# Linear attention and a gated long convolution on one core: orbit order split by parity, scoring tiles of 128 columns, last batch stored tile by tile

## The chip, the cores and the metric

The kernel runs on one core of a Trainium2 chip. The metric is device time in microseconds for one launch. The kernel before has a median of 273.19 us over three runs (269.62, 273.19 and 273.72 us). "PE" is TensorE, "PEld" its weight loads, "DVE" VectorE, "ACT" ScalarE, "POOL" GpSimd and "SP" SyncE, whose queue starts DMAs.

## The reference

Eight batches, eight heads, 576 positions, 64 features per head. A linear attention with cosine weighting feeds a gated convolution over the positions:

```python
def phi(x, c, s):
    r = np.maximum(x, 0.0)
    return np.concatenate([r * c, r * s], axis=-1)
q_p, k_p = phi(q, cos_w, sin_w), phi(k, cos_w, sin_w)
kv  = np.einsum('bhsf,bhsd->bhfd', k_p, v)
num = np.einsum('bhsf,bhfd->bhsd', q_p, kv)
den = np.einsum('bhsf,bhf->bhs', q_p, np.sum(k_p, axis=2))[..., None] + 1e-06
x   = (num / den)                       # then [b, 576, 512]
...
x1, x2, x3 = split(x @ w_proj, 3)       # 512 columns each
x2_conv = irfft(rfft(x2, axis=1) * rfft(filter_fft, axis=0), n=576, axis=1)
out = (x1 * x2_conv * x3) @ w_out
```

## The kernel before

**Work of one batch.** POOL's queue loads q, k and v and casts them to fp16 (`load_qk`). DVE makes the rectified, weighted `kp` and `qp` (`emit_phi`), ACT copies v into `va`. `emit_kv` multiplies them per head into `kvs` (128 features by 65 columns, the last for the denominator; 48 matmuls at L519). `emit_qt` transposes `qp` into `qpt`, 128 features by 8 heads by 576 positions: by PE for batches 0 and 1, and from batch 2 on by four DMA transposes on SP's queue (L531).

`emit_num` (L547) is the scoring step. For each pair of heads it writes one PSUM unit. For each head it goes over six tiles of 96 positions; a tile takes every second column of `qpt` from a block of 192 columns as the stationary operand (96 columns) and streams 65 columns of `kvs` (L558). That is 48 matmuls a batch. DVE then adds epsilon, takes the reciprocal and multiplies into `att` (L564, L567, L568).

`emit_fx` (L573) turns the positions into sums over orbits, the first stage of a discrete Fourier transform by hand. The helper `fold` (L581) takes 128 features of one `att` tile as the stationary operand (96 by 128) and streams the table `fm` (96 by 192). Two tiles, e = 0 and 1, share 384 columns of a PSUM bank: the view `(g o e)` has e innermost, so each matmul writes 192 values, two apart. There are 24 such matmuls a batch (16 into `fx`, 8 into `fxc`), and ACT casts the sums into the SBUF tile `fx` (L593, L601).

`emit_x2`, `emit_dft` (L609, L625) project the second third, transform it and multiply it by the filter's spectrum; `emit_gate` (L647) projects the first and last third, and DVE multiplies them into `g` (L671); `emit_inv` (L680) transforms back, ACT casts into `eq` (L693). `emit_y` (L698) combines even and odd halves on DVE: per 128 features four `eo` instructions of 128 by 144 (L705), two of 128 by 288 (L708, L709), and a product with `g` (L710). `emit_out` (L717) multiplies by `w_out` in five tiles of 128 positions (L728), scales into `os` (ACT at L733; in the last batch ACT at L735 and DVE through the helper at L100) and stores rows to DRAM (L748): nine stores a batch of up to 96 rows, on SP's queue, in the last two batches partly on ACT's.

**Order of the work.** The code is written as a pipeline (L841 to L896): iteration b scores and folds batch b+1, transforms and gates batch b, and stores batch b-1. A scheduler orders each engine's list at build time from there. All PSUM results share one pool of four units of two banks (`unit`, L64): a matmul group that starts a new unit waits until ACT or DVE has emptied an earlier one.

**Tables.** `emit_fm`, `emit_fwd_tables` and the index row `sr_i` compute the fold table and the transform tables on the chip at the start; their formulas follow the order in which `fx` holds the positions.

Of the kernel before, what the change touches and what calls it, by code (L numbers as in the profile page):

```python
# [11 lines left out]
FP32 = mybir.dt.float32  # L12
FP16 = mybir.dt.float16
# [4 lines left out]
def kernel(  # L18
# [8 lines left out]
    out: bass.AP,  # L27
):


# [60 lines left out]
    feo = setupp.tile([NP, 2, 3, DM], FP16, tag="feo", name="feo")  # L91
    qpt_buf = [consts.tile([128, NH, S], FP16, tag=f"qpt{i}", name=f"qpt{i}") for i in range(1)]
    va_buf = [consts.tile([NP, NH, NJ, 66], FP16, tag=f"va{i}", name=f"va{i}") for i in range(2)]
# [242 lines left out]
    def emit_fwd_tables():  # L336
# [3 lines left out]
        tsc(half, p, 47.5, AL.is_gt)  # L340
        u = small("u16")
        rnd(u, p, 1.0 / 16.0, -15.0 / 32.0)
        j = small("jr")
        nc.vector.scalar_tensor_tensor(
            out=j, in0=half, scalar=-3.0, in1=u, op0=AL.mult, op1=AL.add
        )
        w = small("w2s")

        tsc(w, p, 12.0, AL.mult, 1.0, AL.add)
        nc.vector.scalar_tensor_tensor(out=w, in0=u, scalar=-192.0, in1=w, op0=AL.mult, op1=AL.add)  # L350
        nc.vector.scalar_tensor_tensor(out=w, in0=j, scalar=2.0, in1=w, op0=AL.mult, op1=AL.add)
        tn = setupp.tile([NP, 3, NP], I32, tag="tn_big", name="tn_fwd")
# [86 lines left out]
    def emit_h(bls):  # L439
# [8 lines left out]
        for bl in bls:  # L448
# [16 lines left out]
            nc.vector.tensor_copy(out=h3[:, bl, 2], in_=h3[:, bl, 1])  # L465
        if 2 not in bls:
            return
        u = unit("h_nyq")
        for j in range(3):
            nc.tensor.matmul(  # L470
                u[0:1, 0], alt[:, j % 2 : j % 2 + 1], feo[:, 0, j], start=(j == 0), stop=(j == 2)
            )
        nc.scalar.activation(out=h3[0:1, 0, 2], in_=u[0:1, 0], func=AF.Copy, scale=1.0 / S)

# [52 lines left out]
    def emit_qt(b, hp):  # L527
        qp, qpt = qp_t[b], qpt_buf[0]
        hsl = slice(2 * hp, 2 * hp + 2)
# [17 lines left out]
    def emit_num(b, hp, wm=0):  # L547
# [6 lines left out]
        for hh in range(2):  # L554
            h = 2 * hp + hh
            for t in range(NT):
                c0 = 2 * NP * (t // 2) + t % 2
                nc.tensor.matmul(  # L558
                    u[0:NP, hh, ds(t * 65, 65)], qpt[:, h, c0 : c0 + 2 * NP - 1 : 2],
                    kvs[:, h // 4, ds((h % 4) * 65, 65)], start=True, stop=True,  # L560
                )
# [13 lines left out]
    def emit_fx(b, cs=range(NC), wm=0):  # L575
# [5 lines left out]
        def fold(dst, j, c):  # L581
            for e in range(2):
                nc.tensor.matmul(  # L583
                    dst[:, 0:384].rearrange("p (g o e) -> p g o e", o=8, e=2)[:, :, :, e],
                    att[:, 2 * j + e, ds(c * 128, 128)], fm[0:NP], start=True, stop=True,
                )
# [60 lines left out]
    def emit_gate(b, c):  # L647
# [22 lines left out]
        for hf in range(2):  # L670
            mark["g", b, c] = nc.vector.tensor_tensor(  # L671
                out=(g[:, c, 0:HS] if hf == 0 else g[:, c, HS:S][:, ::-1]).rearrange(
                    "p (j i o) -> p j i o", j=3, i=6
                ),
                in0=x3s[:, hf, 0:HS].rearrange("p (i j o) -> p j i o", i=6, j=3),
                in1=x1s[:, hf].rearrange("p (i j o) -> p j i o", i=6, j=3),
                op=AL.mult,
            )
# [19 lines left out]
    def emit_y(b, c):  # L698
        eq, y, g = moe[b]["eq", c], moe[b]["y"], moe[b]["g"]
        eo = late["p"].tile([128, 2, HS], FP16, tag="eo", bufs=2, name=f"eo{b}_{c}")  # L700
        eoh = eo.rearrange("p a (j x) -> p a j x", j=3)
        eqj = eq.rearrange("p a b (j x) -> p a b j x", j=3)
        for x, op in ((0, AL.add), (1, AL.subtract)):
            for a in range(2):
                nc.vector.tensor_tensor(  # L705
                    out=eoh[:, a, :, ds(48 * x, 48)], in0=eqj[:, a, 0], in1=eqj[:, a, 1], op=op
                )
        nc.vector.tensor_tensor(out=y[:, c, 0:HS], in0=eo[:, 0], in1=eo[:, 1], op=AL.add)  # L708
# [5 lines left out]
    OG = ((0, 1), (2, 3), (4,))  # L714
    OL = ((4,), (0, 1), (2, 3))

    def emit_out(b, grps=OG):  # L717
        y = moe[b]["y"]
        ov = out[b].rearrange("(p j) n -> j p n", j=6)
        for grp in grps:  # L720
            ng = len(grp)
            os_ = late["p"].tile(
                [128, ng, DM], FP32, tag=f"os{ng}", bufs=2 * ng, name=f"os{b}_{grp[0]}"
            )
            u = unit(f"out{b}_{grp[0]}")
            for x, t in enumerate(grp):
                for c in range(NC):
                    nc.tensor.matmul(  # L728
                        u[:, x], y[:, c, ds(OT[t], 128)], wo16[:, c],
                        start=(c == 0), stop=(c == NC - 1),  # L730
                    )
            if b < B - 1:
                nc.scalar.mul(out=os_[:, 0 : len(grp)], in_=u[:, 0 : len(grp)], mul=OUTSC)  # L733
            else:
                nc.scalar.mul(out=os_[:, 0], in_=u[:, 0], mul=OUTSC)  # L735
                if len(grp) > 1:
                    tsc(os_[:, 1], u[:, 1], OUTSC, AL.mult)
            for t in grp:
                lo, hi_ = (OT[t], OT[t] + 128) if t < 4 else (512, 576)
                x = lo  # L740
                while x < hi_:
                    jb = x // NP
                    e = min(hi_, (jb + 1) * NP)
                    p_a, p_b = x - jb * NP, e - jb * NP
                    src = os_[x - OT[t] : e - OT[t], t - grp[0]]
                    dst = ov[jb, p_a:p_b]
                    q_ = nc.scalar if b >= B - 2 and t % 2 == 1 else nc.sync
                    q_.dma_start(out=dst, in_=src)  # L748
                    x = e

# [90 lines left out]
    for b in range(1, B + 1):  # L841
# [47 lines left out]
        for x in range(4):  # L889
            if b >= 1 and x < 3 and (b != B - 1 or x > 0):  # L890
                emit_out(b - 1, ((OG if b < B else OL)[x],))
        if n + 1 < B:
# [34 lines left out]
```

## Time and profile before

| What | Value |
|---|---|
| median of three runs | 273.19 us (269.62 to 273.72) |
| the profiled execution: its own time, and its span | 272.69 us, 270.9 us |
| PE busy | 248.9 us, 92% of the span, 2265 matmuls |
| PE weight loads busy | 180.0 us, 66% |
| DVE busy | 219.5 us, 81%, 790 instructions |
| ACT busy | 188.0 us, 69%, 268 instructions |
| POOL busy | 35.5 us, 13% |
| chain that ended last | PE 80%, DVE 10%, ACT 4%, DMA 3% |
| granted PE clock, mean over the span | 0.98 |

The profile is one execution. Busy time is an average over stages with different limits, so the stages have to be read one by one: the chain of waits tells which engine's work follows itself without a gap, and the table of windows gives the busy time of each engine in a stretch. Matmuls overlap each other, so the mean duration of one is longer than its share of the time: what a matmul costs on the chain is the length of its stretch divided by the number in it.

### The profile page before, as it was taken

What the parts mean: (1) busy time and instruction counts of PE and PEld (TensorE: products, weight loads), DVE (VectorE), ACT (ScalarE), POOL (GpSimd) and SP (SyncE); (2) the same over time, 40 slices, a digit from 0 to 9 for tenths busy, and PEclk for the clock granted to TensorE, in tenths of its full rate; (3) what the DMA queues carried; (4) which work ended last, traced back from release to release, by engine and by line L of the source; (5) the groups of instructions that cost most, each with busy time, mean ns of one, the idle gap of its engine ahead of it and who ended that gap; (6) DMA issues with size and microseconds to landing.
All of it is one profiled execution on the core that took longest, in us unless ns stands there. A gap on an engine that the chain in (4) does not pass through costs nothing.

```text
span 270.9 us, 6009 instructions
## 1 busy us (share of the span) xinstructions
PE 248.9 (92%) x2265; PEld 180.0 (66%) x2265; DVE 219.5 (81%) x790; ACT 188.0 (69%) x268; POOL 35.5 (13%) x59
## 2 busy tenths in 40 slices
PE   0389898999889999999999999999999999999991
PEld 0267576756767866785778677867786778756830
DVE  7677889899799879988798969896996597546951
ACT  2244599999778859766886778576966466767630
POOL 8516011413110310030012011000000000000000
PEclk9995999999999999999999999999999999999997
DMA  5999996899997489949996999816600600062045
GB/s 73 184 207 203 207 199 92 95 212 189 142 144 121 47 193 132 196 73 167 175 154 101 150 182 159 124 31 178 142 2 1 173 4 2 0 174 70 12 116 155
DMA packets 60205, 33.75 MB, mean 125 GB/s; under 512 B 39504, under 2 KB 55376, under 8 KB 60176
## 3 DMA queue, kind: packets, MB, share of 16 engines
q0 software_dynamic: 26000, 16.85, 46.0%
q1 hardware_dynamic: 33536, 15.47, 27.5%
q10 hardware_dynamic: 640, 1.05, 1.3%
q8 instruction: 17, 0.28, 0.4%
q14 instruction: 12, 0.10, 0.1%
HBM read 33.69 MB, written 9.44 MB: 159 GB/s over the span
## 4 chain that ended last, share of the span: by engine, by line
PE 80%; DVE 10%; ACT 4%; DMA 3%; issue 1%; POOL 0%; POOLq 0%; ACTq 0%
PE x L658 20%; PE x L618 15%; PE out L728 11%; PE fx L583 7%; PE num L558 6%; PE kv L519 4%; PE dft L633 4%; PE fxc L583 3%; PE inv L689 2%; PE inv L690 2%; DMA vraw<-in_v_dram 2%; DVE kp L102 2%; PE h_ps L457 2%; DVE eo L705 2%; ACT fx L593 1%; PE qt L539 1%
## 5 line engine op out<-in xcount | busy, mean ns | idle before, releaser
L658 PE MATMUL x<-fx,wp 128*128 128x288 f16 x512 | 68.3, 287 | 0.6 <-ACT fx L593 0.6
L658 PEld LDWEIGHTS <-wp 128*128 128x128 f16 x512 | 51.6, 101 | 14.0
L618 PE MATMUL x<-wp,fx 128*96 128x512 f16 x192 | 46.2, 381 | 1.0 <-DVE qpt L545 0.9
L593 ACT CAST fx<-fx 128x768 f16<-128x768 f32 x32 | 25.3, 797 | 21.3 <-PE fx L583 21.3
L728 PE MATMUL out<-wo,y 128*128 128x512 f16 x160 | 36.0, 379 | 0.7 <-DVE y L710 0.7
L623 ACT ACTIVATE x2f<-x 96x1024 f16<-96x1024 f32 x24 | 24.6, 1024 | 15.1 <-PE x L618 15.1
L618 PEld LDWEIGHTS <-fx 128*96 128x96 f16 x192 | 22.0, 123 | 15.4 <-issue 1.3
L139 ACT COPY va<-vraw 96x768 f16<-96x768 f16 x32 | 25.2, 832 | 8.7 <-DMA vraw<-in_v_dram 8.7
L568 DVE TENSOR_TENSOR att<-num,rcp 96x768 f16<-96x768 f32 x32 | 30.3, 947 | 0.2
L583 PEld LDWEIGHTS <-att 96*128 96x128 f16 x192 | 24.2, 128 | 9.3 <-DVE att L568 2.5
L583 PE MATMUL fx<-fm,att 96*128 96x192 f16 x128 | 26.6, 364 | 1.5 <-DVE att L568 1.5
L728 PEld LDWEIGHTS <-y 128*128 128x128 f16 x160 | 15.3, 98 | 18.2 <-DVE y L710 1.2
L705 DVE TENSOR_TENSOR eo<-eq 128x144 f16<-128x144 f16 x128 | 22.9, 225 | 5.5 <-ACT eq L693 5.3
L671 DVE TENSOR_TENSOR g<-x,x1s 128x288 f16<-128x288 f32 x48 | 20.4, 448 | 7.9 <-PE x L658 6.9
L558 PEld LDWEIGHTS <-qpt 128*96 128x96 f16 x384 | 21.6, 126 | 6.4 <-issue 2.6
L635 ACT CAST xf<-dft 96x1024 f16<-96x1024 f32 x24 | 24.1, 1006 | 2.1 <-ACT x1s L664 1.9
L519 PE MATMUL kv<-va,kp 96*128 96x65 f16 x384 | 16.6, 199 | 9.6 <-ACT va L139 7.6
L733 ACT ACTIVATE os<-out 128x1024 f32<-128x1024 f32 (+1 forms) x21 | 17.8, 880 | 10.7 <-PE out L728 10.7
L664 ACT CAST x1s<-x 128x576 f16<-128x576 f32 x32 | 20.5, 642 | 4.9 <-PE x L658 2.3
L519 PEld LDWEIGHTS <-kp 96*128 96x128 f16 x384 | 15.3, 102 | 12.7 <-DVE kp L102 10.7
L558 PE MATMUL num<-kvs,qpt 128*96 128x65 f16 x384 | 21.4, 211 | 1.4 <-DVE rcp L567 0.7
L638 DVE TENSOR_TENSOR m<-xf,h 96x1024 f16<-96x1024 f16 x24 | 16.3, 678 | 5.4 <-ACT xf L635 4.7
(191 smaller groups left out, 421.7 us busy)
## 6 DMA issues: line engine op xcount, KB each, us to landing
out_dram<-os SPq DMA_DIRECT2D x22, 192.0 KB, 2.6
kraw<-in_k_dram POOLq DMA_DIRECT2D x7, 576.0 KB, 9.2
vraw<-in_v_dram POOLq DMA_DIRECT2D x7, 576.0 KB, 8.0
out_dram<-os SPq DMA_DIRECT2D x20, 128.0 KB, 2.4
qraw<-in_q_dram POOLq DMA_DIRECT2D x8, 288.0 KB, 5.4
qraw<-in_q_dram POOLq DMA_DIRECT2D x12, 144.0 KB, 5.4
wp<-in_moe_w_proj_dram POOLq DMA_DIRECT2D x3, 512.0 KB, 11.6
out_dram<-os SPq DMA_DIRECT2D x22, 64.0 KB, 2.0
```

The lines of the kernel that those rows point to most:

```text
L139: nc.scalar.copy(out=va_buf[b % 2][:, hs, :, 0:D], in_=raw_t[(b, "v")][:, hs].rearrange("p h (j d) -> p h j d", j=NJ),)
L519: nc.tensor.matmul(u[:, h // 4, ds((h % 4) * 65, 65)], kp[:, j, h].rearrange("p a b -> p (a b)"), va[:, h, j, 0:65], start=(j == 0), stop= ...
L558: nc.tensor.matmul(u[0:NP, hh, ds(t * 65, 65)], qpt[:, h, c0 : c0 + 2 * NP - 1 : 2], kvs[:, h // 4, ds((h % 4) * 65, 65)], start=True, sto ...
L568: mark["att", b, hp] = nc.vector.tensor_tensor(out=att[:, :, ds(hp * 128, 128)].rearrange("p t (h d) -> p h t d", h=2), in0=nv[:, :, :, 0: ...
L583: nc.tensor.matmul(dst[:, 0:384].rearrange("p (g o e) -> p g o e", o=8, e=2)[:, :, :, e], att[:, 2 * j + e, ds(c * 128, 128)], fm[0:NP], s ...
L593: nc.scalar.copy(out=fx[:, c, :, 0:32].rearrange("p g (j o) -> p j g o", j=2), in_=u[:, :, 0:384].rearrange("p j (g o) -> p j g o", o=16),)
L618: nc.tensor.matmul(u[0:NP, comp], fx[:, c, ds(comp * 6 + 2 * bl, 2)].rearrange("p a b -> p (a b)"), wp16[:, c, ds(DM, DM)], start=(c == 0) ...
L623: mark["x2f", b, bl] = nc.scalar.mul(out=x2f[:, bl], in_=u[0:NP], mul=X2SC)
L635: mark["xf", b, bl] = nc.scalar.copy(out=xf, in_=u[0:NP])
L658: nc.tensor.matmul(u[:, hf, 0:HS], wp16[:, i, ds(w * DM + c * 128, 128)], fx[:, i, ds(12 + 6 * hf, 6)].rearrange("p a b -> p (a b)"), star ...
L705: nc.vector.tensor_tensor(out=eoh[:, a, :, ds(48 * x, 48)], in0=eqj[:, a, 0], in1=eqj[:, a, 1], op=op)
L728: nc.tensor.matmul(u[:, x], y[:, c, ds(OT[t], 128)], wo16[:, c], start=(c == 0), stop=(c == NC - 1),)
```

## The change

**Parity.** The orbit order of the positions is split by parity. In `fold` the view becomes `(g e o)`: each matmul writes 24 runs of 8 adjacent values. `fx` keeps its size, but its 48 places per group stand in another order, so the tables' formulas, the views of `g`, `eo` and the rows of the output follow it. With the new order the four `eo` instructions of 128 by 144 become two of 128 by 288, and an output tile's rows go to DRAM in runs of at most 48 rows (stride 12) where they went in runs of at most 96 (stride 6): 15 stores a batch where there were 9.

**Scoring.** `qpt` becomes one flat tile, and `emit_num` takes 128 stationary columns (every second one, so the last 32 belong to the next tile or the next head) in place of 96, except for the last two tiles of a pair's second head: 40 of the 48 matmuls of a batch have 128 columns and 8 keep 96. The 32 further rows of PSUM that they write are not read.

**Last batch.** Each of the five output tiles of batch 7 gets its own PSUM unit, its own scaling on DVE (`osl`, five buffers) and its own stores, on SP's and ACT's queues, in the order 0 to 4 (before: tile 4 first, then pairs, scaled by ACT and DVE in turn). Batch 6's tiles 2 to 4 store partly by POOL's queue in place of ACT's. The `os` tiles of the other batches have half as many buffers.

**Small things.** The matmuls for the Nyquist row `h_nyq` stand behind the first block of `emit_h` in place of the last; `sr_i` is made by three POOL instructions in place of one; `emit_fwd_tables` has two more column instructions on DVE.

```diff
@@ emit_iotas
-        iota("sr_i", [NP, QS], lambda t: [(t, [[2, 3], [12, NP // 2]], 1, 0)])
+        iota("sr_i", [NP, QS], lambda t: [
+            (t[:, ds(j * 48, 48)], [[12, 2], [192, 3], [24, 8]], 2 * j + 1, 0) for j in range(3)
+        ])
...
@@ emit_num
-                c0 = 2 * NP * (t // 2) + t % 2
+                m = NP if hh and t >= 4 else 128
+                c0 = h * S + 2 * NP * (t // 2) + t % 2
                 nc.tensor.matmul(
-                    u[0:NP, hh, ds(t * 65, 65)], qpt[:, h, c0 : c0 + 2 * NP - 1 : 2],
+                    u[0:m, hh, ds(t * 65, 65)], qpt[:, c0 : c0 + 2 * m - 1 : 2],
                     kvs[:, h // 4, ds((h % 4) * 65, 65)], start=True, stop=True,
                 )
...
@@ fold
-                    dst[:, 0:384].rearrange("p (g o e) -> p g o e", o=8, e=2)[:, :, :, e],
+                    dst[:, 0:384].rearrange("p (g e o) -> p g e o", e=2, o=8)[:, :, e],
                     att[:, 2 * j + e, ds(c * 128, 128)], fm[0:NP], start=True, stop=True,
...
@@ emit_gate
-                    "p (j i o) -> p j i o", j=3, i=6
+                    "p (t i o) -> p t i o", t=6, i=6
                 ),
-                in0=x3s[:, hf, 0:HS].rearrange("p (i j o) -> p j i o", i=6, j=3),
-                in1=x1s[:, hf].rearrange("p (i j o) -> p j i o", i=6, j=3),
+                in0=x3s[:, hf, 0:HS].rearrange("p (i t o) -> p t i o", i=6, t=6),
+                in1=x1s[:, hf].rearrange("p (i t o) -> p t i o", i=6, t=6),
...
@@ emit_y
-            for a in range(2):
-                nc.vector.tensor_tensor(
-                    out=eoh[:, a, :, ds(48 * x, 48)], in0=eqj[:, a, 0], in1=eqj[:, a, 1], op=op
-                )
+            nc.vector.tensor_tensor(
+                out=eoh[:, :, :, x], in0=eqt[:, :, 0], in1=eqt[:, :, 1], op=op
+            )
...
@@ emit_out
+                if last and x:
+                    u = unit(f"out{b}_{t}")
...
+                if last:
+                    tsc(os_[t][:, 0], u[:, x], OUTSC, AL.mult)
...
+                while pos < hi_:
+                    m = pos // 48
+                    e = min(hi_, (m + 1) * 48)
+                    k0 = pos - m * 48
+                    r = 6 * (m % 2) + m // 2
+                    q_ = nc.sync
+                    if m % 2 == 1 and (last or (b == B - 2 and t > 1)):
+                        q_ = nc.scalar if last else nc.gpsimd
+                    q_.dma_start(out=ov[r, k0 : k0 + e - pos], in_=sv[pos - OT[t] : e - OT[t]])
+                    pos = e
```

The order of PE's matmuls in the pipeline's middle is the same in both kernels. Two places move. The first is SP's queue in the middle of the pipeline: the DMA transposes of one batch and, behind them, the stores of another (`os_0`, `os_2` and `os_4` are its scaled tiles). Before:

```order
L531 DMA_TRANSPOSE qpt_90<-qp_2458 128x12x96 x4
L748 DMA out_dram<-os_0_2488 96x512
L748 DMA out_dram<-os_0_2488 32x512
L748 DMA out_dram<-os_0_2488 64x512 x2
L748 DMA out_dram<-os_2_2503 32x512
L748 DMA out_dram<-os_2_2503 96x512 x2
L748 DMA out_dram<-os_2_2503 32x512
L748 DMA out_dram<-os_4_2518 64x512
```

Changed:

```order
L538 DMA_TRANSPOSE qpt_90<-qp_2452 128x12x96 x4
L760 DMA out_dram<-os_0_2483 48x512 x2
L760 DMA out_dram<-os_0_2483 32x512
L760 DMA out_dram<-os_0_2483 16x512
L760 DMA out_dram<-os_0_2483 48x512 x2
L760 DMA out_dram<-os_0_2483 16x512
L760 DMA out_dram<-os_2_2501 32x512
L760 DMA out_dram<-os_2_2501 48x512 x4
L760 DMA out_dram<-os_2_2501 32x512
L760 DMA out_dram<-os_4_2518 16x512
L760 DMA out_dram<-os_4_2518 48x512
```

The four transposes of the next batch now stand behind 15 stores where they stood behind 9.

The second place is the end of the program, on ACT and DVE; `os_..._41xx` and `os_..._42xx` are the scaled tiles of batch 7, `os_2_4126`/`os_4_4141` (changed: `os_2_4116`/`os_4_4133`) those of batch 6. ACT before:

```order
L733 ACTIVATE os_4_4141<-out_4_4142 128x512
L748 DMA out_dram<-os_2_4126 96x512
L748 DMA out_dram<-os_2_4126 32x512
L735 ACTIVATE os_4_4181<-out_4_4182 128x512
L735 ACTIVATE os_0_4189<-out_0_4190 128x512
L748 DMA out_dram<-os_0_4189 64x512 x2
L735 ACTIVATE os_2_4205<-out_2_4206 128x512
L748 DMA out_dram<-os_2_4205 96x512
L748 DMA out_dram<-os_2_4205 32x512
```

ACT changed:

```order
L747 ACTIVATE os_4_4133<-out_4_4132 128x512
L760 DMA out_dram<-os_0_4166 48x512
L760 DMA out_dram<-os_1_4173 48x512
L760 DMA out_dram<-os_1_4173 16x512
L760 DMA out_dram<-os_2_4187 32x512
L760 DMA out_dram<-os_2_4187 48x512
L760 DMA out_dram<-os_3_4194 48x512
L760 DMA out_dram<-os_4_4207 48x512
```

ACT only issues stores there now, and the five scalings stand on DVE behind the last `y`:

```order
L716 TENSOR_TENSOR y_4048<-eo_3_4159 128x288
L717 TENSOR_TENSOR y_4048<-eo_3_4159 128x288
L718 TENSOR_TENSOR y_4048<-y_4048,g_3970 128x576
L102 TENSOR_SCALAR os_0_4166<-out_0_4165 128x512
L102 TENSOR_SCALAR os_1_4173<-out_1_4172 128x512
L102 TENSOR_SCALAR os_2_4187<-out_2_4186 128x512
L102 TENSOR_SCALAR os_3_4194<-out_3_4193 128x512
L102 TENSOR_SCALAR os_4_4207<-out_4_4206 128x512
```

Before, DVE had two of them (`os_0` and `os_2`'s second halves), each behind ACT's half of the same tile.

More of the change, by code (lines that the diff above doesn't have):

```diff
@@ L91 @@
     feo = setupp.tile([NP, 2, 3, DM], FP16, tag="feo", name="feo")
-    qpt_buf = [consts.tile([128, NH, S], FP16, tag=f"qpt{i}", name=f"qpt{i}") for i in range(1)]
+    qpt_buf = [consts.tile([128, NH * S], FP16, tag=f"qpt{i}", name=f"qpt{i}") for i in range(1)]
     va_buf = [consts.tile([NP, NH, NJ, 66], FP16, tag=f"va{i}", name=f"va{i}") for i in range(2)]
@@ L465, in emit_h @@
             nc.vector.tensor_copy(out=h3[:, bl, 2], in_=h3[:, bl, 1])
[L466 to L473, printed above, removed]
+            if bl > 0:
+                continue
+            u = unit("h_nyq")
+            for j in range(3):
+                nc.tensor.matmul(
+                    u[0:1, 0], alt[:, j % 2 : j % 2 + 1], feo[:, 0, j], start=(j == 0), stop=(j == 2)
+                )
+            nc.scalar.activation(out=h3[0:1, 0, 2], in_=u[0:1, 0], func=AF.Copy, scale=1.0 / S)
     kp_t, qp_t, kvs_t, att_t, fx_t, xt_t = {}, {}, {}, {}, {}, {}
```

62 lines of the change are left out of this document (28 added, 34 removed).

## The prediction

> **What bounds the kernel now.** I read the table of windows first, to see which engine fills which stretch, with the stretches cut where the chain of waits changes its engine. The columns are the length, then busy time and instructions of PE, PEld, DVE, ACT and POOL, the granted PE clock, the DMA share and GB/s.
>
> ```profile
> 30.70:44.70 14.00, 12.41 (x125) 10.07 (x126) 13.18 (x51) 12.39 (x21) 1.54 (x2) 1.00 1.05 157
> 44.70:62.00 17.30, 17.30 (x160) 11.18 (x160) 15.87 (x48) 16.91 (x27) 4.49 (x5) 1.00 1.10 159
> 71.00:77.27 6.27, 4.86 (x106) 4.33 (x104) 5.73 (x26) 5.71 (x9) 0.00 (x0) 1.00 0.83 145
> 77.27:99.47 22.20, 22.20 (x202) 16.55 (x200) 21.41 (x75) 17.19 (x25) 2.82 (x4) 1.00 0.76 112
> 99.47:239.28 139.81, 139.81 (x1284) 103.16 (x1282) 115.52 (x372) 100.76 (x135) 8.72 (x12) 1.00 0.65 109
> ...
> 127.74:156.00 28.26, 28.26 (x267) 20.92 (x266) 24.76 (x81) 20.84 (x28) 3.60 (x5) 1.00 1.00 148
> ```
>
> From 77 to 239 us PE has no idle time, at full clock. One batch takes 28.26 us there; DVE is busy for 24.76 and ACT for 20.84 of it. So PE's list is the time of that stretch, and a nanosecond off it is a nanosecond off the kernel until DVE's 24.76 or ACT comes up. The DMA share of 1.00 is no bound: POOL holds each load back until a buffer comes free, as this row of the waits between 99.47 and 239.28 shows (total, times, longest), and no engine waits for a DMA there.
>
> ```profile
> POOL kraw L134 <- DVE qp L102: 21.7, 3, 7.2
> ```
>
> The first 77 us and the last 18 are mixed. The chain of waits then gives the price of each step of one batch (start, length, what):
>
> ```profile
> 127.74 1.74 PE x L618 x8
> 129.48 1.08 PE num L558 x24
> 137.94 0.43 PE dft L633 x2
> 138.37 0.65 PE fx L583 x4
> 139.02 1.96 PE x L658 x16
> 150.16 4.32 PE out L728 x20
> 154.48 1.53 PE kv L519 x48
> ```
>
> Three of these lie on one line: 512 streamed columns cost 1.74/8 = 217 ns (L618), 288 cost 1.96/16 = 122.5 ns (L658), so a column costs 0.42 ns and 192 columns should cost 82 ns. The folds (L583) with their 192 columns cost 0.65/4 = 163 ns, twice that. They are the only matmuls whose PSUM writes are not adjacent. The scoring (L558) is the second exception: 1.08/24 = 45 ns with 65 columns, where `kv` with the same 65 columns takes 1.53/48 = 32 ns. The groups show the difference between those two:
>
> ```profile
> L558 PEld LDWEIGHTS <-qpt 128*96 128x96 f16 x384 | 21.6, 126 | 6.4 <-issue 2.6 <-ACT qpt L544 0.3
> L519 PEld LDWEIGHTS <-kp 96*128 96x128 f16 x384 | 15.3, 102 | 12.7 <-DVE kp L102 10.7
> ```
>
> A weight load of 128 columns takes 102 ns and one of 96 columns takes 126 ns: the wider one is faster. With so few columns to stream, the load sets the pace.
>
> **The folds.** 24 matmuls a batch go from 163 ns to, at best, 82: 24 x 81 = 1.94 us off PE per batch. The other bound is no gain (163), if a run of 8 followed by a gap counts like a step of two. No row shows a matmul that writes runs. I take 82, since a write of 8 adjacent values is nearer to the contiguous rows than to a pattern in which no two are adjacent, and since a factor of exactly two at step two speaks for pairs of adjacent values being written at once.
> [...]
>
> **The scoring.** 40 of 48 matmuls a batch go from 45 ns to 32 if the wide load is as fast with every second column as `kv`'s with adjacent ones: 40 x 13 = 0.51 us. The strided load of 96 columns in the row above (126 ns) is no slower than adjacent ones of the same width, as in this row:
>
> ```profile
> L618 PEld LDWEIGHTS <-fx 128*96 128x96 f16 x192 | 22.0, 123 | 15.4 <-issue 1.3 <-ACT fx L601 0.5
> ```
>
> so the step itself costs at most 3 ns, and I take 32. The other bound: the load grows with its columns, 45 x 128/96 = 60 ns, and the scoring costs 0.6 us more a batch.
> [...]
>
> **DVE.** Two `eo` instructions of 128x288 replace four of 128x144, 16 to 8 a batch. From the timeline, on one stretch:
>
> ```profile
> 73.20 0.52 DVE L705 TENSOR_TENSOR eo<-eq 128x144 f16<-128x144 f16 x3
> 73.63 0.31 DVE L708 TENSOR_TENSOR y<-eo 128x288 f16<-128x288 f16 x1
> 73.85 0.30 DVE L709 TENSOR_TENSOR y<-eo 128x288 f16<-128x288 f16 x1
> ```
>
> Three small ones take 0.43 us from start to the next start, 0.143 each; a large one takes 0.22. Four times (0.57 - 0.44) is 0.53 us off DVE a batch. The views of `g` (L671) go from 18 runs of 16 values to 36 of 8:
>
> ```profile
> L671 DVE TENSOR_TENSOR g<-x,x1s 128x288 f16<-128x288 f32 x48 | 20.4, 448 | 7.9 <-PE x L658 6.9 <-ACT x1s L664 1.1
> ```
>
> No row shows what a run costs; between nothing and one element's time each (448/288 = 1.6 ns), 18 more runs in 8 instructions cost 0 to 0.2 us a batch. I take nothing: it would lie in DVE's idle time, which falls from 3.5 us a batch to 28.26 - 2.45 - (24.76 - 0.53) = 1.6 us. That cover is thin; without it each such tenth lands on PE.
>
> **What takes some back.** ACT empties PSUM just in time around the scoring:
>
> ```profile
> 132.34 1.02 ACT L623 ACTIVATE x2f<-x 96x1024 f16<-96x1024 f32 x1 [0.35 <-PE x L618]
> 133.26 0.82 ACT L139 COPY va<-vraw 96x768 f16<-96x768 f16 x1
> 133.98 1.01 ACT L635 CAST xf<-dft 96x1024 f16<-96x1024 f32 x1
> 134.88 0.84 ACT L139 COPY va<-vraw 96x768 f16<-96x768 f16 x1
> 135.62 1.03 ACT L623 ACTIVATE x2f<-x 96x1024 f16<-96x1024 f32 x1
> ...
> 133.64 1.91 PE L618 MATMUL x<-wp,fx 128*96 128x512 f16 x8
> ```
>
> The third `x2` group starts at 133.64, in the unit that ACT frees at 132.34 + 1.02 = 133.36: 0.28 us to spare, and ACT has no gap from 132.34 to 137. PE's two scoring groups before it shrink by 2 x 10 x 13 = 0.26 us, so that spare time is used up and the next copy, which ACT starts only when its own list lets it, comes late by up to that much. I put 0.2 us a batch back: 1.94 + 0.51 - 0.2 = 2.25 us. Everything queued behind the late copy on ACT shifts with PE, not more.
>
> **SP's queue.** 15 stores replace 9, ahead of the transposes:
>
> ```profile
> 127.82 1.50 SPq L748 DMA_DIRECT2D out_dram<-os  x3
> 130.05 14.00 SPq L531 DMA_TRANSPOSE qpt<-qp  x4
> 152.97 4.01 SPq L748 DMA_DIRECT2D out_dram<-os  x8
> ```
>
> A store takes SP 0.5 us, so the stores take 7.5 us where they took 4.5, then 14 us of transposes: 21.5 of a batch's 25.8 us. The transposes start some 2 to 3 us later against PE. Before, the last one is issued by 144 and the scoring that reads it starts after 157.7; some 7 us stay even if it lands well behind its issue. So nothing for this, and the halved `os` buffers cost nothing either, as each is reused a batch later.
>
> **The start.** PE's folds of batch 0 lie on the chain, some at half clock:
>
> ```profile
> 21.35 1.14 PE fx L583 x3
> 23.86 1.28 PE fxc L583 x4
> 30.71 0.84 PE fx L583 x4
> ```
>
> Halving the first two saves 1.2 us, the others up to 0.7. But from 30.7 to 44.7 DVE is busy for 13.18 of 14.00 us, so only what comes before 30.7 counts: 1.6 with the neighbouring fold and scoring. From 44.7 to 62 PE is full and holds 48 scoring matmuls: 0.5. The folds of batch 1 (62 to 67) wait for ACT's copies: nothing. I take 2.0 (bounds 0 and 3.4). From 71.00 to 77.27 DVE's `y` of batch 0 is the chain: 0.5.
>
> **Batch 1's stretch** (77.27 to 99.47) has DVE at 21.41 of 22.20. PE saves 1.94 + 0.13, DVE 0.5: DVE becomes the limit for a while, and part of that is regained in the next batch. I take 1.5.
>
> **The end.** The last rows of the timeline:
>
> ```profile
> 260.72 0.46 DVE L710 TENSOR_TENSOR y<-y,g 128x576 f16<-128x576 f16 x1
> 261.23 3.84 PE L728 MATMUL out<-wo,y 128*128 128x512 f16 x17 [0.66 <-DVE y L710]
> 264.01 0.69 DVE L100 TENSOR_SCALAR os<-out 128x512 f32<-128x512 f32 x1 [2.84 <-ACT os L735]
> 264.74 1.12 ACTq L748 DMA_DIRECT2D out_dram<-os  x2
> 265.99 0.60 ACT L735 ACTIVATE os<-out 128x512 f32<-128x512 f32 x1 [2.00 <-DMA out_dram<-os]
> 266.62 0.69 DVE L100 TENSOR_SCALAR os<-out 128x512 f32<-128x512 f32 x1 [1.91 <-DMA out_dram<-os]
> 267.34 0.81 ACTq L748 DMA_DIRECT2D out_dram<-os  x2
> ```
>
> The matmuls end at 265.1, but ACT spends 264.74 to 265.86 on issuing two stores, so its scaling starts at 265.99, DVE's half follows it, and the last store is issued at 267.7, 6.5 us after the last `y` (261.2); the span ends 3.2 us later. In the change DVE's 0.69 us per tile keep up with PE's 4 x 0.216 = 0.87, so the last scaling ends 3.7 + 0.7 = 4.4 us after the last `y`, and one store on each queue follows: 2.0 us earlier. The cheaper `eo` bring the last `y` 0.5 us forward. Sum 2.4 with something for a slower store (bounds 1.0 and 3.2).
>
> **The sum** is made against the profiled execution, 272.69 us with a span of 270.9, half a microsecond under the median of 273.19. Start 2.0 + 0.5, batch 1's stretch 1.5, five batches between 99.47 and 239.28 at 2.25 = 11.25, end 2.4: 17.65 us, which is 255.0 for that execution and 255.5 against the median.
>
> **Rivals.** (a) *DVE becomes the engine that sets the pace.* For it: only 1.6 us idle a batch remain, and DVE's list also waits for PE and ACT in places. Against it: DVE's waits for PE shrink as PE gets faster. If 1 us a batch is lost in the five batches, with a little more in batch 1's stretch, the time is 261. (b) *The new fold pattern is as slow as the old one.* Then five batches give 0.4 each, the start 0.6, DVE 0.5, the end 2.4: about 5.5 us, 267.7. Against it stands the exact factor of two. (c) *The wide load is not fast with a step of two.* Then a batch gains 1.94 - 0.6 = 1.3: 6.5 for five, 0.9 + 1.4 + 0.5 + 2.4 besides, 261.5. (d) *Slower than before: SP's queue becomes the bound.* If a small store cost SP not 0.5 but 1.2 us, 15 of them and the 14.0 us of transposes make 32 us a batch against 28.26 now; five batches lose 3.7 each, less 6 us gained at both ends and in batch 1's stretch: about 285. It decides from the point where the queue passes PE's 25.8, at 0.79 us a store, and makes the kernel slower from about 1.03. Against it: the eleven stores in the rows above took 0.5 us each, with 32 to 96 rows.
>
> **Chances.** Forecast as above 0.65; (a) 0.17; (b) 0.06; (c) 0.10; (d) 0.02. A measurement of this kernel tells about 2% from no change, so faster means below 267.7. The forecast, (a) and (c) are faster (0.92), (b) sits on the border and is split 0.02 to 0.04: faster 0.94, same 0.04, slower 0.02. The range goes from 251.0, where the start gives its 3.4, ACT takes nothing back and the end gives 3.2, to 262.0, which takes in (a) and (c).
>
> **What would show it.** Right: the fold group at about 0.33 us per four in the chain and 24 scoring matmuls at 0.80 to 0.85; weight loads of the scoring near 102 ns; a batch at 26 us with PE still full; DVE at 24.2; no PE wait for a transpose; no ACT scaling between the last stores. Wrong: fold groups still at 0.65 (b), scoring above 1.08 per 24 (c), PE idle before DVE's `att` or `g` (a), or PE waiting for `qpt` behind SP (d).

## The result and the profile after

The changed kernel takes 260.24 us (median of four runs, 259.34 to 262.53) where the kernel before takes 272.78 in the same comparison (269.62 to 273.72). The ratio is 0.959, with a 95% interval of 0.947 to 0.971. The prediction was 255.5 us, in a range of 251.0 to 262.0. The direction is right and the time lies in the range, but only about 12.5 us came where 17.65 were summed. The 5 us between them are what the experiments looked for. (Ratios leave disturbed runs out and medians do not, so the two can differ by about one per cent.)

The profiled execution took 262.53 us with a span of 260.7, the longest of the four. Its stages, cut where the prediction cut them (the first `x2` group of batch 1, of batch 2, and of batch 7):

```profile
77.69:99.45 21.76, 21.74 (x202) 15.67 (x201) 19.01 (x63) 16.40 (x24) 2.03 (x4) 0.94 0.91 137
99.45:228.90 129.45, 128.91 (x1283) 93.18 (x1282) 112.66 (x332) 100.22 (x135) 8.65 (x12) 1.00 0.66 119
228.90:260.70 31.80, 25.14 (x167) 15.52 (x164) 18.82 (x48) 13.75 (x19) 2.03 (x4) 0.95 0.37 107
```

| Stage | before | changed | gained | forecast |
|---|---|---|---|---|
| up to the `x2` group of batch 1 | 77.27 | 77.69 | -0.4 | 2.5 |
| batch 1's stretch | 22.20 | 21.76 | 0.4 | 1.5 |
| five batches | 139.81 | 129.45 | 10.4 | 11.25 |
| the rest | 31.6 | 31.8 | -0.2 | 2.4 |

So the middle came nearly as summed, and both ends gave nothing. The third last column of the first row, the granted clock, is 0.94 where it was 1.00.

**The two cheaper steps are there.** The groups (busy time, mean ns of one, idle before):

```profile
L592 PE MATMUL fx<-fm,att 96*128 96x192 f16 x128 | 16.0, 246 | 2.2 <-DVE att L577 1.6 <-ACT xf L644 0.4 <-ACT fx L602 0.2
L567 PEld LDWEIGHTS <-qpt 128*128 128x128 f16 x320 | 14.3, 100 | 9.0 <-DMA qpt<-qp 3.2 <-issue 2.3 <-ACT qpt L551 0.8
L567 PEld LDWEIGHTS <-qpt 128*96 128x96 f16 x64 | 5.6, 127 | 0.0
L680 DVE TENSOR_TENSOR g<-x,x1s 128x288 f16<-128x288 f32 x48 | 20.4, 447 | 2.3 <-PE x L667 2.3
```

A load of 128 strided columns takes 100 ns, one of 96 takes 127, side by side in one kernel; and `g` with 36 runs of 8 costs 447 ns where 18 runs of 16 cost 448. The chain of waits of a full batch (125.74 to 152.03) and of the last full one (204.62 to 228.90, which has no `kv`) shows what the steps cost on the path:

```profile
127.48 0.79 PE num L567 x24
...
133.44 2.12 PE x L667 x16
...
135.61 0.68 DVE m L647
136.29 0.60 DVE m L648
136.89 0.37 DVE g L680
...
138.36 0.45 issue
138.81 0.68 DVE m L648
```

```profile
204.62 1.74 PE x L627 x8
...
212.32 1.96 PE x L667 x16
...
214.72 0.33 PE fx L592 x4
```

Four folds take 0.33 us (82 ns each) and 24 scoring matmuls 0.79 (33 each), as forecast. But in the full batch the chain leaves PE behind the first gate group and runs through DVE's `m` and `g`, where it was all PE before. The last batch, with less for DVE to do, runs on PE alone and takes 24.28 us; with the 1.53 of `kv` that is 25.81, PE's own list. The full batch takes 26.29. Nearly all of the 0.48 us between them stands in two waits of PE. The first gate group takes 2.12 us for 1.96: its ninth matmul starts at 134.41, behind this copy of ACT, which empties its unit at 134.36:

```profile
133.33 1.03 ACT L632 ACTIVATE x2f<-x 96x1024 f16<-96x1024 f32 x1
```

The other is the second group of the inverse transform, which starts at 144.51, when DVE's last `g` has emptied its unit. The waits of the same batch (total, times, longest) show it on PE's weight loads:

```profile
PEld L698 <- DVE g L680: 0.3, 1, 0.3
```

DVE is not short of time in all; between 99.45 and 228.9 it waits:

```profile
DVE rcp L573 <- PE num L567: 10.8, 5, 3.1
```

That is 2 us a batch ahead of the scoring's end, behind which its work then piles up.

**The start** ends in a wait for the DMA transposes of batch 2:

```profile
62.44 14.32 DMA qpt<-qp
76.80 0.89 PE num L567 x12
77.69 2.99 PE x L627 x8
```

The transpose issued at 62.44 has landed at 76.76, and the `x2` group behind it runs at 2.99/8 = 374 ns a matmul where 1.74/8 = 217 was paid at full clock: the granted clock is 0.50 from 76.68 to 80.09 us, 0.60 on average over the group. **The end**, from the timeline:

```profile
249.77 7.91 SPq L760 DMA_DIRECT2D out_dram<-os  x12
250.37 2.03 POOL L760 DMA_DIRECT2D out_dram<-os  x4 [89.57 <-ACT os L747]
251.57 5.80 ACTq L760 DMA_DIRECT2D out_dram<-os  x7
254.30 0.69 DVE L102 TENSOR_SCALAR os<-out 128x512 f32<-128x512 f32 x1 [0.17 <-PE out L740]
```

The last `y` ends when POOL's row begins, and the last scaling at 254.99, 4.6 us behind it (before: 6.1). The stores are issued until 257.68, and the span ends 5.7 us after the last scaling (before: 270.9 - 267.31 = 3.6).

### The profile page after: what moved, and what is told of

It is laid out like the page before. It is cut to its first block, busy times and chain, and to the rows that moved or that the text cites. A ratio compares the mean times of both kernels' runs of the same rounds, so it can differ in the third digit from the quotient of the medians.

```text
span 260.7 us, 6016 instructions
## 1 busy us (share of the span) xinstructions
PE 233.3 (90%) x2265; PEld 165.5 (63%) x2265; DVE 219.0 (84%) x732; ACT 185.3 (71%) x265; POOL 37.5 (14%) x65
## 4 chain that ended last, share of the span: by engine, by line
PE 59%; DVE 21%; DMA 8%; ACT 7%; issue 2%; POOL 0%; DVEq 0%; POOLq 0%
PE x L627 15%; PE out L740 12%; PE x L667 12%; DMA qpt<-qp 5%; DVE g L680 5%; DVE kp L104 5%; PE kv L526 4%; PE num L567 4%; PE dft L642 3%; DMA vraw<-in_v_dram 2%; PE inv L698 2%; PE inv L699 2%; DVE m L648 2%; PE fx L592 2%; ACT va L141 1%
## 5 line engine op out<-in xcount | busy, mean ns | idle before, releaser
L667 PEld LDWEIGHTS <-wp 128*128 128x128 f16 x512 | 49.6, 98 | 15.0 <-issue 2.1
L627 PE MATMUL x<-wp,fx 128*96 128x512 f16 x192 | 48.3, 395 | 1.1 <-DVE qpt L552 0.9
L627 PEld LDWEIGHTS <-fx 128*96 128x96 f16 x192 | 22.9, 128 | 16.5 <-issue 3.3
L567 PEld LDWEIGHTS <-qpt 128*128 128x128 f16 (+1 forms) x384 | 16.6, 105 | 9.0 <-DMA qpt<-qp 3.2
L713 DVE TENSOR_TENSOR eo<-eq 128x288 f16<-128x288 f16 x64 | 17.4, 298 | 5.6 <-ACT eq L702 5.5
L592 PEld LDWEIGHTS <-att 96*128 96x128 f16 x192 | 16.8, 98 | 6.7 <-DVE att L577 2.4
L567 PE MATMUL num<-kvs,qpt 128*128 128x65 f16 (+1 forms) x384 | 17.3, 199 | 3.6 <-DMA qpt<-qp 2.8
L702 ACT CAST eq<-inv 128x576 f16<-128x576 f32 x32 | 18.3, 670 | 1.5 <-PE inv L699 1.5
```

The source lines that it names most:

```text
L567: nc.tensor.matmul(u[0:m, hh, ds(t * 65, 65)], qpt[:, c0 : c0 + 2 * m - 1 : 2], kvs[:, h // 4, ds((h % 4) * 65, 65)], start=True, stop=True,)
L592: nc.tensor.matmul(dst[:, 0:384].rearrange("p (g e o) -> p g e o", e=2, o=8)[:, :, e], att[:, 2 * j + e, ds(c * 128, 128)], fm[0:NP], star ...
L627: nc.tensor.matmul(u[0:NP, comp], fx[:, c, ds(comp * 6 + 2 * bl, 2)].rearrange("p a b -> p (a b)"), wp16[:, c, ds(DM, DM)], start=(c == 0) ...
L667: nc.tensor.matmul(u[:, hf, 0:HS], wp16[:, i, ds(w * DM + c * 128, 128)], fx[:, i, ds(12 + 6 * hf, 6)].rearrange("p a b -> p (a b)"), star ...
```

## The experiments

Each starts from the changed kernel. Medians scatter by one to two us for reasons that the fourth group of runs shows, so a stage is read from the profile, where a batch in the middle repeats within 0.02 us.

**1. What the folds and the scoring are worth.** Folds two apart again:

```diff
-dst[:, 0:384].rearrange("p (g e o) -> p g e o", e=2, o=8)[:, :, e],
+dst[:, 0:384].rearrange("p (g o e) -> p g o e", o=8, e=2)[:, :, :, e],
```

> The changed kernel, but each fold writes its 192 values two apart again (e innermost), so the positions stand in a wrong order in the fold's result; every instruction, its size and its order stay. Theory (adjacent runs of 8 are what makes the fold cheap, and PE sets most of the pace): four folds take 0.65 us again instead of 0.33, a batch in the middle takes 27.8 to 28.0 us instead of 26.3, and the time is 269 to 272 us, 9 to 12 above the changed kernel's 260. Rival (the gain comes from the scoring and the fewer DVE and end instructions, and the folds were hidden): at most 263 us.

Measured: 272.38 us (267.97 to 275.70), ratio 0.991 [0.984, 0.999] to the kernel before. One batch, and the four folds in it:

```profile
129.84:157.74 27.90, 27.90 (x267) 20.32 (x266) 24.29 (x72) 20.86 (x28) 3.60 (x6) 1.00 0.98 150
```

```profile
142.72 0.65 PE fx L592 x4
```

The rival falls: without the adjacent runs the ratio goes from 0.959 to 0.991, and three quarters of the gain are gone. Now 96 columns in the scoring:

```diff
-                m = NP if hh and t >= 4 else 128
+                m = NP
```

> The changed kernel with 96 stationary columns in all 48 scoring matmuls. 24 of them should take 1.08 us again instead of 0.79, so 0.58 us of PE a batch comes back. Theory A (PE alone sets the pace): each batch grows by 0.58, the time by 3.5 to 4 us, to about 264. Theory B (DVE holds PE up between 135 and 144 us by about 0.4 us a batch): the longer scoring is partly paid from that wait, a batch grows by 0.1 to 0.3 us, and the time by 1 to 2 us, to about 261.5.

Measured: 262.65 us (259.91 to 265.10), ratio 0.957 [0.947, 0.966]. The batch:

```profile
122.23:148.78 26.55, 26.52 (x267) 19.55 (x266) 24.32 (x73) 20.77 (x28) 3.55 (x5) 1.00 1.00 157
```

24 scoring matmuls take 1.07 again, 0.58 us of PE a batch, but the batch grows by 0.26. That is the size of theory B: 0.32 of the scoring's gain had been swallowed by waits. But DVE has only a part of them. In this run's batch the first gate group and the wait for `g` read

```profile
130.46 1.96 PE x L667 x16
```

```profile
PEld L698 <- DVE g L680: 0.2, 1, 0.2
```

so with the longer scoring PE no longer waits for ACT's copies at all (0.15 us at the gate group and 0.05 at the third `x2` group before it), and for DVE about 0.1 less.

**2. Whether DVE holds PE.** The second product of the filter step is left out in batches 2 to 6:

```diff
+            if b < 2 or b > 6:
                 nc.vector.tensor_tensor(out=m2, ...)
+            else:
+                m2 = m1
```

> The changed kernel without the second product (m2) of the filter step in batches 2 to 6, three DVE instructions of about 0.6 us a batch, just where PE waits for DVE; the imaginary part of the filter is left out there. Theory B (PE waits for the units that g and att on DVE empty): these waits go, a batch in the middle takes 25.8 to 25.9 us instead of 26.29, as the last full one already does in 24.28 with its out-of-loop work left off, and the time falls by 1.5 to 2.2 us to about 258.3. Rival (ACT or the scoring's own pace holds PE): period and time unchanged within 0.3 us.

Measured: 261.12 us (256.08 to 261.61); the time did not show the gain. The batch did:

```profile
125.60:151.56 25.96, 25.96 (x267) 18.94 (x266) 22.12 (x69) 20.77 (x28) 3.55 (x5) 1.00 1.03 161
```

0.33 us a batch come back with DVE's work, where 0.4 to 0.5 were expected, and no wait of PE for `g` is left. The remaining 0.15 over PE's 25.81 lies at the first gate group (2.11 us for 1.96 in the chain), behind ACT's `x2f` again; with the folds two apart it is there too, and DVE's wait is not, so 25.96 + 1.94 = 27.90 gives the batch measured there. (25.96 + 0.58 = 26.54 is close to the 26.55 with 96 columns only by luck: there it is DVE that holds PE up, not ACT.) DVE's wait can be relieved with the result kept whole, by letting ACT copy the third factor for two of four column groups:

```diff
-    X3_ACT = ()
+    X3_ACT = (1, 3)
```

> The changed kernel with the third factor of the gate copied to SBUF by ACT for two of four column groups (1 and 3) in all batches, as batches 0 and 1 have it for all; DVE then multiplies from SBUF, about 0.14 us less in each of four instructions a batch, and ACT has 1.3 us more. Theory B (PE waits for units that DVE's g empties): the units come free without DVE, a batch in the middle takes 25.9 to 26.1 us instead of 26.29, the time falls by 1 to 1.5 us. Rival (ACT's list is as tight as DVE's, as its just-in-time copies say): 26.3 or more, no gain or a loss of up to 2 us.

Measured: 258.90 us (257.68 to 262.97), ratio 0.954 [0.947, 0.962].

```profile
125.85:152.00 26.15, 26.15 (x267) 19.01 (x266) 23.54 (x74) 21.82 (x30) 3.57 (x5) 1.00 1.04 161
```

A batch gains 0.13 us, 0.7 over five, less than the 0.2 to 0.4 expected. `g` falls from 448 to 301 ns where ACT copies, as expected, and PE no longer waits for it. But the second group of the inverse transform, whose matmuls follow each other every 0.06 us, now waits for ACT's copy of `fxc`:

```profile
145.48 0.19 PE inv L698
```

**3. The end.** One store of 128 rows for each output tile of batches 6 and 7 (rows in a wrong order):

```diff
+                if b >= B - 2:
+                    q_ = nc.scalar if last and t % 2 == 1 else nc.sync
+                    q_.dma_start(out=out[b, lo:hi_], in_=sv[lo - OT[t] : hi_ - OT[t]])
+                    continue
```

> The changed kernel with one store of 128 rows per output tile in batches 6 and 7, so 8 stores at the end where there are 23, none of them by POOL; the rows of these two batches land in a wrong order. Theory C (the small stores set the end: each one waits until the store eight before it has landed, 2 to 4 us after its issue): no such wait is left, the last store is issued within 0.1 us of the last scaling, the span ends 4 to 4.5 us after the last scaling instead of 5.7, and the time falls by 1.3 to 2 us. Rival (the landing of the last store and the end of the program take those 5.7 us anyway): unchanged within 0.4 us. The transposes at the start are not touched: if batch 2's transposes are late in this profile too, that wait belongs to the change, if not, to the one profiled execution.

Measured: 260.54 us (257.67 to 262.38), ratio 0.951 [0.939, 0.964]. The end of its timeline, span 257.6:

```profile
248.88 5.73 SPq L753 DMA_DIRECT2D out_dram<-os  x6
251.56 2.06 ACTq L753 DMA_DIRECT2D out_dram<-os  x2
253.42 0.69 DVE L102 TENSOR_SCALAR os<-out 128x512 f32<-128x512 f32 x1 [0.17 <-PE out L740]
```

From the last scaling (254.11) to the end are 3.4 us in place of 5.7 (4 to 4.5 were expected): 2.3 us of the profile are the small stores' price. All of it lies ahead of the last store's issue: at 254.14 here, right behind its scaling, and in the changed kernel at 257.30, 2.3 us behind it. The ratio moves that way within its interval; the start, below, moves a time by as much. The waits of SP's queue between 244 and 262 us name what a store of the changed kernel waits for, first there, then here:

```profile
SPq L760 <- DMA out_dram<-os: 2.5, 1, 2.5
```

```profile
SPq L753 <- DVE os L102: 2.9, 3, 1.3
```

In the trace the stores on SP and ACT take turns on eight semaphores (111 to 118), and a store waits until the earlier one on its semaphore has landed: SP's store issued at 255.00 stands behind ACT's of 251.57, which landed at 254.94. With 23 stores, 19 of them on these two queues, SP stands still for 2.5 us in this way; with 8 it never does, and waits for DVE's scalings instead. Taking four of the 19 stores off these queues should then help:

```diff
-                    if m % 2 == 1 and (last or (b == B - 2 and t > 1)):
-                        q_ = nc.scalar if last else nc.gpsimd
+                    if b == B - 2 and t > 1:
+                        q_ = nc.gpsimd
+                    elif m % 2 == 1 and last:
+                        q_ = nc.scalar
```

> The changed kernel with all eight late stores of batch 6 (tiles 2 to 4) on POOL's queue, where four of them were on SP's; the rows are right. Theory C (a store on SP or ACT waits until the one eight before it on these two queues has landed): 15 stores instead of 19 share these eight places, the waits of SP at 252.4 to 255.0 and of ACT at 254.7 to 256.5 shrink, and the span ends 4.5 to 5.0 us after the last scaling instead of 5.7. Rival (POOL's four stores and its final drain set the end): eight of them make it longer than 5.7.

Measured: 259.57 us (258.85 to 261.84), ratio 0.960 [0.953, 0.967]; the last scaling ends at 251.80, the span at 257.5, again 5.7 us apart. Neither expectation holds. The DMA view from 244 us on (KB of one, median us from issue to landing) shows what moved, the changed kernel first, then this run, then the single large stores:

```profile
out_dram<-os SPq DMA_DIRECT2D x6, 96.0 KB, 2.1
out_dram<-os ACTq DMA_DIRECT2D x5, 96.0 KB, 3.3
out_dram<-os POOLq DMA_DIRECT2D x3, 96.0 KB, 3.2
```

```profile
out_dram<-os POOLq DMA_DIRECT2D x5, 96.0 KB, 4.3
out_dram<-os ACTq DMA_DIRECT2D x5, 96.0 KB, 3.2
out_dram<-os SPq DMA_DIRECT2D x4, 96.0 KB, 3.6
```

```profile
out_dram<-os SPq DMA_DIRECT2D x4, 256.0 KB, 2.2
```

The stores on SP and POOL land later than before, those on ACT do not, and SP still waits for landings (2.5 us in three waits); the last store is issued at 254.16, 2.4 us behind the last scaling. 256 KB in one store land in 2.2 us. So the many small stores set the end, through their waits for each other's landings, and moving four of them to POOL does not help. Whether it is their number, their size or their rows 12 apart in DRAM stays open, since the large stores changed all three (and left POOL's queue out).

**4. The start.** The changed kernel once more:

> The changed kernel once more, to see which of its losses come back in another execution. Theory V (the late transposes of batch 2, which held PE up by 2.8 us at 74 us, are a matter of the one execution): in this profile they land by 66 to 72 us or so, no wait or a shorter one stands there, and the span is 256.5 to 258.5 us. Theory P (the change itself delays them): a wait of 2.5 us or more again, span near 260. The halved clock for 3.4 us near 62 to 66 us should come back in either case if it follows from the gaps between the folds of batch 1; median 259 to 261 us.

Measured: 259.88 us (259.15 to 263.20), ratio 0.960 [0.954, 0.966]; the profiled execution took 259.73 with a span of 257.4. The `x2` groups of batch 1, 2 and 7 start at 75.69, 96.21 and 225.62, so the stages gain 1.6, 1.7, 10.4 and -0.2 us, 13.5 together. The first two are the forecast's 2.5 and 1.5 less 0.7. There is still a wait for the transposes, but of 2.1 us, and the clock holds behind it (1.00 from 75.69 to 96.21). Neither theory is right as written: the shorter wait and the span are theory V's, the landing at 75.1 us is not. The half clock near 62 us, expected in either case, did not come back (1.00 from 58 to 66 us). Then 96 columns again and the kernel before again, for their starts alone:

> The changed kernel with 96 stationary columns in the scoring, once more, for its start alone. Of nine profiles of the changed kernel and its variants, only this variant had batch 2's last DMA transpose landed at 64.5 us; the eight with 128 columns had it at 74 to 78 us. Theory P (the wider scoring goes with slow transposes): below 68 us again. Theory V (chance from one execution to the next): 70 us or later.

> The kernel before, once more, for its start alone: batch 2's last DMA transpose landed at 66.2 us in its first profile. Theory P (the change brings the slow transposes): 64 to 69 us again, no wait of PE for them. Theory V (chance): 72 us or later here too, if not in this execution then in one of the two.

Measured, in one execution each: 262.24 us with the last transpose of batch 2 landed at 65.1, and 276.50 us with it landed at 78.6. The chain of the kernel before, second profile:

```profile
64.59 14.02 DMA qpt<-qp
79.39 3.43 PE x L618 x8
```

It has the same kind of wait (2.5 us), and behind it `x2` matmuls of 3.43/8 = 429 ns, twice the 217 of full clock (the granted clock is 0.91 on average from 78 to 98 us). Its span is 274.7, 3.8 us above the first profile. So late transposes come without the change too. The profile of before that the prediction rests on was one without them. They came in one of two profiles of before, in none of two of the changed kernel with 96 columns, and in all nine with 128 columns in which DMA transposes batch 2. One of four against nine of nine suggests that the wide scoring makes them likelier; no run shows how it could, and it stays open.

The half clock behind the wait, and the one that the first profile shows earlier, follow gaps in PE's work. From 74 to 77 us PE is busy for 0.04, 0.00 and 0.20 of each microsecond, ahead of and into the half clock from 76.68 on. Slices of 1 us of the changed kernel's first profile, and of the one with folds two apart (PE's busy time behind the comma, the granted clock third from last):

```profile
60.00:61.00 1.00, 0.60 (x7) 0.39 (x5) 1.00 (x4) 1.00 (x2) 0.00 (x0) 1.00 1.26 172
61.00:62.00 1.00, 0.60 (x7) 0.36 (x5) 1.00 (x4) 1.00 (x3) 0.32 (x1) 1.00 1.31 177
...
63.00:64.00 1.00, 1.00 (x4) 0.36 (x3) 1.00 (x4) 1.00 (x3) 1.00 (x2) 0.51 1.38 175
...
66.00:67.00 1.00, 1.00 (x5) 0.57 (x4) 0.93 (x5) 0.01 (x1) 0.70 (x1) 0.78 1.47 130
```

```profile
61.00:62.00 1.00, 1.00 (x8) 0.73 (x7) 1.00 (x4) 1.00 (x2) 0.00 (x0) 1.00 1.29 166
```

These are the folds of batch 1, which wait for ACT's copies. Slow folds fill that time; fast ones leave PE idle for 0.4 of a microsecond, and here the granted clock was 0.50 for 3.4 us, from 63.0 to 66.4. To fill the gaps:

```diff
-        emit_fx(1, (c,))
+        emit_fx(1, (c,), 1)
```

> The changed kernel with one more matmul of 512 columns on unused data ahead of the folds of each group of batch 1 (four in all, 0.22 us each), where PE is busy for only 0.6 of three microseconds between ACT's copies. Theory G (those gaps make the granted clock fall to one half for a window of 3.4 us, which costs 1.7 us of work): the clock stays at 1.00 from 56 to 74 us, the kv group of batch 2 starts 1 to 1.7 us earlier, and the time falls by about 1.5 us. Rival (the clock falls for another reason, or ACT sets the pace there): the half clock stays near 62 to 66 us, or the kv group starts no earlier than 69.5 us.

Measured: 261.71 us (258.30 to 263.64), ratio 0.962 [0.953, 0.971]. The clock stays at 1.00 from 58 to 68 us, and the `kv` group of batch 2 starts at 69.0 us, 0.8 earlier than in the first profile (69.87), where 1 to 1.7 were expected. The second profile of the changed kernel had no half clock there either and started it at 68.9, so this run alone shows nothing, and the time did not fall. The count over the profiles of all runs speaks for theory G: near 62 us the clock fell in five of eight with fast folds and these gaps open, in none of five with slow folds or filled gaps. With so few it is no proof, and three profiles with the same gaps kept the clock, so something else decides as well. Lastly the transposes of batch 2 on PE:

```diff
-    DMA_QT = 2
+    DMA_QT = 3
```

> The changed kernel with batch 2 transposed by PE instead of by DMA (48 transposes, about 3 us of PE, and eight copies by ACT and DVE). If the late DMA transposes are what holds PE up at 74 us and lets the clock fall at 76 us, both go, and the kv group of batch 3 starts at 94 to 96 us in every execution; the 3 us of transposes take most of that back, so the time stays within 1.5 us of the changed kernel's 260. If PE still waits there, or the clock still falls, something else holds it, and the time rises by 2 to 4 us.

Measured: 262.59 us (261.88 to 264.13), ratio 0.966 [0.959, 0.974]. The wait for the DMA is gone and the clock holds at 76 us (0.98 on average from 70 to 78), but PE waits 2.2 us for DVE's copies of the transposes, the clock fell at 63.5 us behind that longer gap (0.60 on average from 62 to 70 us), and the `kv` group of batch 3 starts at 99.4 us in place of 94 to 96. The median lies 2.4 us above the changed kernel's; the late transposes are cheaper than this cure.

**5. Both harmless edits together** (ACT's copies for groups 1 and 3, and the filled gaps).

> The changed kernel with the two edits of earlier runs that keep the result whole and did no harm: ACT copies the third gate factor for column groups 1 and 3, and one more matmul on unused data stands ahead of each group of batch 1's folds. By the sum of what each showed, a batch in the middle takes 26.15 us instead of 26.28 (0.7 us over five), and the clock does not fall near 62 us (1.1 us where it otherwise does): 258 to 259 us, ratio to the kernel before 0.950 to 0.957. If late transposes and the clock's windows decide, it lies at 260 like the changed kernel, and the profile shows a wait for qpt near 74 us with a half clock behind it.

Measured: 260.16 us (258.15 to 261.38), ratio 0.960 [0.954, 0.967]. A batch takes 26.15 us and the clock holds near 62 us (the matmuls of the inverse transform follow each other every 0.06 us from 64 us on, as at full clock), as summed, but the time stays at 260 where 258 to 259 were summed. Its profile has the late transposes (75.8 us) with a half clock at 76.6 (`x2` matmuls of 3.19/8 = 399 ns), as the expectation's last sentence has it. No version beats the changed kernel by what these measurements can tell.

## Why the prediction came out as it did

- **The folds**, 1.94 us a batch: right to the digit with DVE's wait out of the way (27.90 - 25.96); with it, 27.90 - 26.29 = 1.61 remain. Runs of 8 cost what contiguous columns cost: 82 ns for 192 columns, and 122.5 for 288 contiguous ones, 0.43 ns a column in both. Rival (b) is refuted.
- **The scoring**, 0.51 a batch: 0.58 on PE, of which the batch kept 0.26. The load of 128 strided columns is fast (100 ns), so rival (c) is refuted.
- **What takes some back**, 0.2 a batch for ACT: right in mechanism and size. PE waits 0.05 us at the third `x2` group and 0.15 at the gate group behind it, both for ACT's `x2f`, and neither wait is there when the scoring is slow again.
- **DVE**: busy 24.3 us a batch, forecast 24.2. The step that failed is that a nanosecond off PE is one off the kernel "until DVE's 24.76 or ACT comes up". It compares busy totals, and PE waited for DVE although DVE's total stayed below PE's. It is not `g`'s price that failed (447 ns as before), but the cover. DVE's 2 idle us stand before the scoring ends, and between 135 and 144 us its `m`, `g` and `kp` follow each other without a gap, until PE's inverse transform waits for the unit that the last `g` empties. That is rival (a), with its sign of PE idle before `g`, at a third of its price: 0.33 us a batch. Together the five batches gave 10.4 of 11.25.
- **The start and batch 1's stretch**, 2.5 and 1.5: 1.6 and 1.7 in the profile whose clock holds (1.00 from 58 to 66 us and from 75.7 to 96.2), 0.7 short together. "The folds of batch 1 (62 to 67) wait for ACT's copies: nothing" was incomplete: the time freed there is idle time, and in five of eight profiles the granted clock halved behind it, in the first for 3.4 us (the `kv` group of batch 2 started about 1 us later there than in the second). For the transposes of batch 2 the prediction has no term at all. Its chain up to 77.27 was read from one execution in which they landed early; the kernel before has late ones too, and then PE waits for them.
- **The end**, 2.4: nothing. The scalings did what was said (4.6 us behind the last `y`, forecast 4.4), and the last `y` came 0.4 us earlier after its `x2` group. The step that failed is "one store on each queue follows". The last of 23 small stores is issued 2.3 us behind its scaling, held up by waits for earlier landings, and the end falls 5.7 us behind the last scaling where it was 3.6: that puts 2.1 us back. The price per store on SP's queue (0.5 us; 7.39 for 15 in the middle) was right; that a store there also waited for an earlier one to have landed (2.5 us) was missed.
- **SP's queue in the middle**, rival (d): refuted, no engine waits for a transpose after batch 2.
- **The range**: its lower end of 251.0 does not follow from the terms named for it. 255.5 less 1.4 at the start, 1.0 for ACT in five batches and 0.8 at the end is 252.3.

The forecast's error of 5 us is thus 2.6 at the end, 0.9 in the five batches, and the rest in the start, which differs from one execution to the next. The time lies in the part of the range that was kept for rivals (a) and (c), but more for the end than for a reason of theirs.

## What to carry to other kernels

When an engine that sets the pace gets faster, look at where the others' idle time lies, not how much they have in all: DVE had 2 us a batch to spare and still held PE up. Splitting a transfer into more pieces cost nothing here in the middle and 2.3 us at the end, where nothing follows to cover it, and the price lay in waits for landings (2.5 us on SP's queue) rather than in issue time. A stage that waits on a copy gained nothing from faster matmuls, and its gaps may have slowed PE's clock (busy for 0.60 to 0.80 of a microsecond, then a clock of 0.50).

## What the runs showed of the hardware

- A matmul that wrote 192 fp32 values to PSUM in runs of 8 took 82 ns (0.33 us for four), 0.43 ns a column, as one that wrote 288 contiguous ones did (122.5 ns); at a step of two the 192 took 163 ns (0.65 us for four).
- A weight load of 128 columns at a step of two took 100 ns (mean of 320), one of 96 columns at the same step 127 ns (mean of 64), in one kernel.
- Near 62 us the granted clock fell to 0.50 for 3.4 us (63.0 to 66.4), after stretches in which PE was not idle but busy for 0.60, 0.60 and 0.80 of each microsecond, in the changed kernel's first profile. It fell behind the same gaps in five profiles of eight; what decides it stays open.
- The DMA transposes of batch 2 took very different times in one and the same kernel: before, they were issued from 50.5 and 50.4 us on, and the last one landed at 66.2 us in one profile and at 78.6 in the other. From 44 to 62 us, where POOL's casting loads run beside them, the DMA share was 1.08 and 1.18, at 153 and 106 GB/s. What decides it stays open.
